# Turning y by a transposing transfer within SBUF, a stretch ahead, in place of TensorE transposes

## The chip, the core and the metric

The kernel runs on one core of one Trainium2 chip. The metric is the device time of one execution in microseconds. An execution's time is a little longer than the span of its instructions.

## The reference, cut to what matters

There are 8 batches, 5696 tokens and 128 channels. First comes a causal long convolution by FFT; its result is the y (and later x) of the second half. The second half turns y into phases, mixes over the tokens with two 5696 x 5696 matrices, and ends with a small channel product:

```
y     = irfft(rfft(x, 2S) * rfft(h, 2S))[:, :S]
theta = y @ w_theta
zr, zi = y * cos(theta), y * sin(theta)
u     = y + w_tok_r @ zr + w_tok_i @ zi        (the sums run over the tokens, per batch and channel)
out   = u + relu(u @ w_ch)
```

## The kernel before, in words

**Stages.** The first part, to about 400 us, does the FFT convolution and stores y with the channels on the partitions (`yt_hbm`). The second part mixes. A token tile is 128 tokens (45 tiles, the last with 64), and a *half tile* is one tile with 4 of the 8 batches: 128 x 512 values. The sum over the source tokens is cut in two passes. Pass 0 uses the tokens of tiles 0 to 21, pass 1 those of tiles 22 to 43; tile 44 is added at the end of pass 1's sums. After pass 0 the sums go to `cp_hbm` in HBM, and pass 1 loads them again (`addend`, L1091), adds its own, and puts out results.

**Pairs, products, stretches.** Output tiles are worked on in pairs (tt and 22 + tt), each with two halves, by seven products (`ORDER`: M3, M4, M5, M2, M1, M7, M6) in the manner of Strassen. Pair 0, and in pass 0 also pair 1, use four plain products; the lone last tile (`tt is None`) has its own short form. A pair's sum over 11 blocks j of source tokens is cut into four *stretches* of 3, 3, 3 and 2 blocks. In a stretch TensorE runs the seven products in turn (L1396: 6 matmuls for each block count of 3, 4 for 2). VectorE has made their weights before: it turns weights from a ring of six buffers (L972, `wt`) and adds or subtracts turned ones (L981, `out`). At the end of a pair VectorE adds the seven products into four tiles `c` (L1403, twelve additions), while it already makes the weights of the next pair's first stretch. GpSimd issues the weight loads into the ring (L669), each group once VectorE has read the buffer that it replaces.

**Background items.** Pass 1 needs the phases of tiles 22 to 44. They are made during pass 0, one half tile in each of the first three stretches of a pair, from pair 2 on. The list `spread` holds them as triples of functions; `bg_phase` (L989 to 1008) makes one for each half tile: tiles 24 to 33, 22, 23, 44, then 34 to 43, two halves each, 46 in all. After them come 12 items that turn left-over weights (`bg_left`), and in pass 1 the outputs (`u_stage`). Of a phase item
- `load` brings yT (channels on the partitions) from `yt_hbm`: SP, L995;
- `first` turns it with four TensorE transposes into a PSUM tile `tpz` (L1000), copies that with ScalarE into `yb` (L1002), and stores it to `y2_hbm` (L1003);
- `second` calls `phases_b`: four matmuls from yT to `theta_ps` (L552), ScalarE copies and sines (L554, L555, L572, L573, L576), VectorE's rounding (L556), VectorE's products of sine and cosine with `yb` (L587, L588), and four stores of z to `z_hbm` (SP, L611).

`yb` lies in the single buffer that `yt_room` gives (the profile calls it `ring`), so one y at a time is there. `bg_left` and `u_stage` use the same buffer. The PSUM tile `misc` is shared by `tpz`, `theta_ps`, `utp` and `v`.

**Outputs.** In pass 1 `u_stage` treats one finished half tile: ScalarE copies c to `ub` (L1049), SP turns it with a transposing transfer within SBUF (`dma_start_transpose`, L1052), TensorE multiplies by `w_ch` into `v` (L1063), VectorE adds (L1065), SP stores (L1068). The four last ones of the run are turned with TensorE instead (L1056, L1058).

**What sets the order.** `aside(first_of, second_of)` (inside the loop over the stretches) is called after each product and runs the `first` of the next item, then the `load` of the item after the next one, or the `second` of the current item. In Strassen stretches (L1420) `first` follows product 1, and `second` follows product 4 in pass 0, and product 6, or product 0 of the next stretch, in pass 1. Each engine executes its instructions in order; the framework's scheduler chooses that order ahead of time for TensorE, ScalarE and SP, and for VectorE outside of a few hand-ordered sections. SP issues all stores and most loads named here, in one queue.

**Pass change.** At the end of pass 0 the b tiles are loaded again from `z_hbm` and combined on VectorE (L880). Pass 1 starts with pair 0 (plain), then the lone last tile (L1273, four short stretches), then pair 1. The outputs of pair 0 and of the lone tile are the first five `u_stage` items.

Of the kernel before, what the change touches and what calls it, by code (L numbers as in the profile page):

```python
# [23 lines left out]
def kernel(  # L24
# [13 lines left out]
    P = 128  # L38
# [899 lines left out]
    def open_mixing():  # L938

        nonlocal bp, cp, wlp, ybp  # L940
        xa.close()
        bp, cp, wlp, ybp = (ctx.enter_context(tc.tile_pool(name=name, bufs=bufs, reuse_waits="tile"))
                            for name, bufs in (("bpool", 1), ("cpool", 1), ("wlpool", 2), ("ybpool", 3)))
        load_b(0, NJ - 2, bp)
        sides["cs"] = [addend(0, n, t, h) for n, (t, h) in enumerate(((0, 1), (22, 0), (0, 0), (22, 1)))]
        load_b(0, NJ - 1, bp)
        spread.extend(bg_phase(t, h) for t in list(range(24, 34)) + [22, 23, 44] + list(range(34, 44)) for h in range(2))
        spread.extend(bg_left(g) for g in range(0, NT, 4))
        spread[0][0]()
        spread[1][0]()  # L950

    for j in range(NJ):
        owed += [(j, k, lambda j=j, k=k: sum_ops(bts_of[0][j])[k]()) for k in range(5)]
# [35 lines left out]
    def bg_phase(t, h):  # L989
        st = {}  # L990
        m = min(P, S - t * P)

        def load():
            st["yT"] = yT = ybp.tile([P, 4, P], BF16, tag="yb", name="yT")
            nc.sync.dma_start(yT[:, :, :m], yt_hbm[:, 4 * h:4 * h + 4, t * P:t * P + m])  # L995

        def first():
            tpz = mps.tile([P, 4, P], BF16, tag="misc", name="tpz")
            for b in range(4):
                nc.tensor.transpose(tpz[:m, b, :], st["yT"][:, b, :m], ident_bf)  # L1000
            st["yb"] = yb = yt_room()
            nc.scalar.activation(yb[:m], tpz[:m], AF.Copy)  # L1002
            nc.sync.dma_start(half(y2_hbm, t, h)[:m], yb[:m].rearrange("p b d -> p (b d)"))  # L1003

        def second():
            phases_b(t, st["yb"], 4 * h, 4, st["yT"][:, :, :m], cp, mps, "misc", nc.vector,
                     tags=where_bg["tags"], m=m)
        return load, first, second

    def bg_left(g):  # L1010

# [28 lines left out]
            nc.sync.dma_start(wl_hbm[:, g:g + n, :m], wls[:, :n, :m])  # L1040
        return load, first, nothing

    def u_stage(ti, h, c, m):
        st = {}

        def first(tags=("misc", "misc", None)):
            st["tags"] = tags
            ub = ybp.tile([P, 4, D], BF16, tag="yb", name="ub")
            nc.scalar.activation(ub[:m].rearrange("p b d -> p (b d)"), c[:m], AF.Copy)  # L1049
            if not tags[2]:  # L1050
                st["uts"] = uts = yt_room()
                nc.sync.dma_start_transpose(uts, ub.rearrange("p b d -> p (b d)"))  # L1052
                return
            utp = mps.tile([P, 4, P], BF16, tag=tags[0], name="utp")
            for b in range(4):
                nc.tensor.transpose(utp[:, b, :m], ub[:m, b, :], ident_bf[:m, :m])  # L1056
            st["uts"] = uts = cp.tile([P, 4, P], BF16, tag=tags[2], name="uts")
            nc.scalar.activation(uts[:, :, :m], utp[:, :, :m], AF.Copy)  # L1058

        def second():  # L1060
            v = mps.tile([P, 512], F32, tag=st["tags"][1], name="v")
            for b in range(4):
                nc.tensor.matmul(v[:m, b * D:(b + 1) * D], st["uts"][:, b, :m], w_ch_sb,  # L1063
                                 start=True, stop=True)
            nc.vector.scalar_tensor_tensor(c[:m], v[:m], 0.0, c[:m],  # L1065
                                           op0=ALU.max, op1=ALU.add)
            for h_, p0, p1 in (((0, 0, 64), (1, 64, P)) if ti == NT - 1 else ((h, 0, m),)):
                nc.sync.dma_start(  # L1068
                    bass.AP(tensor=out.tensor, offset=out.offset + ti * P * D + 4 * h_ * S * D,
                            ap=[[D, p1 - p0], [S * D, 4], [1, D]]),  # L1070
                    c[p0:p1].rearrange("p (b d) -> p b d", b=4))
        return nothing, first, second
# [36 lines left out]
    def finish(p, ti, h, c, m=P):  # L1109
        if p == 0:  # L1110
            nc.sync.dma_start(half(cp_hbm, ti, h)[:m], c[:m])
        else:
            spread.append(u_stage(ti, h, c, m))

    zl_of = {0: None}

# [82 lines left out]
    for i, (k, p, tt, j0, s0, nj) in enumerate(stretches):  # L1199
# [40 lines left out]
                in_place(j)  # L1240
        if woven:
            nxt, step = nxt
        def aside(first_of, second_of):
            nonlocal second
            if first_of and spread and (p == 1 or (tt > 1 and not end_of_pair)):
                where_bg["tags"] = ("c2", "c3") if j0 + s0 == TJ else ("red", "mag")
                _, first, second = spread.pop(0)
                first()
                if len(spread) > 1:
                    spread[1][0]()  # L1250
            if second_of and second is not None:
                second()
                second = None

        if tt is None:
            if p:
                aside(False, True)
                aside(True, False)
            if first_of_pair:
                q = M1 if p else M3  # L1260
                ps = mps.tile([P, 512], F32, tag=f"m{q}", name=f"m{q}")
                c_last = addend_last(p)
            a1, a2, sa = a
            terms = ((sa, M2, a2, M4), (a1, M3, sa, M5))
            for j in range(nj):
                jj = j0 + s0 + j
                for r in range(2):
                    b = [x[:, r, :] for x in bts[jj]]
                    st_ = jj == 0 and r == 0
                    sp_ = jj == NJ - 1 and r == 1 and zl is None  # L1270
                    for k_ in range(2):
                        for h, t in enumerate(terms):
                            nc.tensor.matmul(ps[64 * h:64 * h + 64], t[2 * k_][:, j, :64, r], b[t[2 * k_ + 1]],  # L1273
                                             start=st_ and k_ == 0, stop=sp_ and k_ == 1)
            if p:
                for f in {0: (lambda: safe(NJ - 2),), TJ: (lambda: safe(NJ - 1),),
                          2 * TJ: (lambda: in_place(NJ - 2), lambda: in_place(NJ - 1))}.get(j0 + s0, ()):
                    f()
            if end_of_pair:
                if zl is not None:  # L1280
                    wl = wl_room()
                    nc.sync.dma_start(wl[:, :64], wl_hbm[:, NT - 1, :64])
                    for h in range(2):
                        nc.tensor.matmul(ps[64 * h:64 * h + 64], wl[:, :64], zl[h], start=False, stop=True)
                c, c0 = c_last
                nc.vector.tensor_add(c, c0, ps)
                finish(p, NT - 1, 0, c)
            continue
# [54 lines left out]
        if classic:  # L1343
            for n in range(4):
                for j in range(nj):
                    last = product(a, j0 + s0 + j, j, n, range(2))
                    if p == 0 and (n * nj + j) % 4 != 3:
                        sum_some(1)
                    if p == 0 and (n * nj + j) % 3:
                        y_some(1, last)  # L1350
                if end_of_pair and n % 2:
                    (c12, z12), (c21, z21), (c11, z11), (c22, z22) = cs
                    out_of = (((c11, z11, 0), (c12, z12, 1)), ((c21, z21, 2), (c22, z22, 3)))[n // 2]
                    for h, (c, z, m_) in enumerate(out_of):
                        if p:
                            nc.tensor.matmul(ms[m_], wl[n // 2], zl[h], start=False, stop=True)
                            nc.vector.tensor_tensor(c, z, ms[m_], op=add)
                            continue
                        if n == 1:
                            nc.tensor.matmul(ms[m_], ident_bf, z, start=False, stop=True)  # L1360
                        else:
                            for b in range(4):
                                nc.tensor.matmul(ms[m_][:, b * D:(b + 1) * D], z[:, b, :], ident_bf,
                                                 start=False, stop=(b == 3))
                        nc.scalar.activation(c, ms[m_], AF.Copy)
                aside(n == 0, n == 2 + p)
            if end_of_pair and woven:
                for n_ in range(7):
                    step(n_)
# [6 lines left out]
        else:  # L1376
# [14 lines left out]
            for n, q in enumerate(ORDER):  # L1391
# [9 lines left out]
                if end_of_pair:  # L1401
# [15 lines left out]
                    if woven:  # L1417
                        for n_ in {1: (0, 1), 2: (2,), 3: (3,), 4: (4,), 5: (5,), 6: (6,)}.get(n, ()):
                            step(n_)
                aside(n == 1, n == (6 if p and i + 1 < len(stretches) else 4) or p and n == 0)  # L1420
        if not end_of_pair:
            continue
        if i + 1 == len(stretches):
# [35 lines left out]
```

## Time and profile before

| | us |
|---|---|
| three runs, median (lowest to highest) | 1995.17 (1993.44 to 1997.12) |
| the profiled execution | 1982.45 |
| its span | 1980.2 |
| TensorE busy in the span | 1897.3 (96%) |
| VectorE busy | 1546.0 (78%) |
| ScalarE busy | 593.9 (30%) |
| GpSimd busy | 976.5 (49%) |
| pass 0's background items, first to last L1000 | 462.8 to 987.2 |
| one pair in pass 0, by its first theta matmul | 34.58 |

The profile lists instructions by source line, the engine, what is written and read, a count, and a duration; views of the trace give timelines, waits and landings of transfers. PE is TensorE's matmuls, PEld its weight loads, DVE is VectorE, ACT ScalarE, POOL GpSimd, and SPq the queue of SyncE. "[0.35 <-PE m]" behind a row means that the engine was idle for 0.35 us before it and that a matmul ended the wait. Matmuls overlap in the records, so their spacing tells more than their duration.

### The profile page before, as it was taken

The numbers are of one execution on the slowest core, as the hardware profiler recorded it, in microseconds if no ns is written. First come the engines' busy times: TensorE is split into PE (matmuls) and PEld (weight loads), VectorE is DVE, ScalarE is ACT, GpSimd is POOL, SyncE is SP. The second block draws the span as 40 slices with busy tenths as digits, with TensorE's granted clock in tenths as the row PEclk, the third lists the DMA queues.
The fourth block names the chain that finished last, engine by engine and source line by source line (L and its number), as shares of the span: only waits on it lengthen the run. The fifth ranks groups of instructions, "written<-read, shape, count | busy, mean of one in ns | idle before, by whom it ended". The sixth has DMA issues, their size and how long they took to land.

```text
span 1980.2 us, 40436 instructions
## 1 busy us (share of the span) xinstructions
PE 1897.3 (96%) x15247; PEld 1043.2 (53%) x15417; DVE 1546.0 (78%) x2855; ACT 593.9 (30%) x875; POOL 976.5 (49%) x1746
## 2 busy tenths in 40 slices
PE   5899998899999999999999997999999999999998
PEld 5799997544444444444444443444444444444444
DVE  8978787876888888888877677677687776777767
ACT  6999997812233333323310000000010000000001
POOL 8636414444453544536475645344535445354451
PEclk9999999999999999999999999999999999999999
DMA  9999959999898998989999899798989989899895
GB/s 110 79 102 145 102 113 243 261 224 167 176 178 173 175 174 159 186 170 178 172 167 162 139 300 174 111 168 142 171 151 170 164 144 165 148 165 172 144 168 115
DMA packets 534067, 323.13 MB, mean 163 GB/s; under 512 B 230311, under 2 KB 494663, under 8 KB 532887
## 3 DMA queue, kind: packets, MB, share of 16 engines
q0 software_dynamic: 322160, 156.41, 63.6%
q1 hardware_dynamic: 204544, 150.37, 28.5%
q10 hardware_dynamic: 7168, 13.76, 2.0%
q8 instruction: 121, 1.98, 0.4%
q14 instruction: 74, 0.61, 0.1%
HBM read 354.37 MB, written 90.29 MB: 225 GB/s over the span
## 4 chain that ended last, share of the span: by engine, by line
PE 63%; DMA 8%; DVE 5%; issue 2%; POOL 1%; SPq 0%; ACT 0%; DVEq 0%; ACTq 0%
PE m L1396 57%; PE m L1308 3%; DMA out_dram<-c 3%; DVE c L1403 2%; DMA c<-cp_hbm 1%; DMA b<-z_hbm 1%; DMA ring<-ub 1%; DVE wt L972 1%; PE v L1063 1%; PE m L1273 1%; PE m L1400 1%; PE tpz L1000 0%; PE misc L1308 0%; POOL ring L669 0%; PE theta_ps L552 0%
## 5 line engine op out<-in xcount | busy, mean ns | idle before, releaser
L669 POOL DMA_DIRECT2D ring<-in_moe_w_tok_i_dram x720 | 389.4, 552 | 660.5 <-DVE wt L972 571.0
L972 DVE STREAM_TRANSPOSE wt<-ring 128x384 f32<-128x384 f32 (+2 forms) x720 | 355.6, 521 | 124.0 <-PE m L1396 58.4
L669 POOL DMA_DIRECT2D ring<-in_moe_w_tok_r_dram x720 | 388.6, 553 | 118.0 <-DVE wt L972 39.7
L1396 PE MATMUL m<-b,wt 128*128 128x512 bf16 x1601 | 386.4, 380 | 4.1 <-DVE wt L972 1.7
L1049 ACT ACTIVATE ub<-c 128x512 bf16<-128x512 f32 x88 | 55.3, 630 | 768.9 <-DVE c L1403 659.4
L1403 DVE TENSOR_TENSOR c<-c,m 128x512 f32<-128x512 f32 x412 | 267.1, 670 | 21.7 <-DMA c<-cp_hbm 21.7
L1396 PEld LDWEIGHTS <-wt 128*128 128x128 bf16 x1804 | 173.3, 98 | 198.8 <-DVE wt L972 4.2
L139 POOL DMA_DIRECT2D x<-in_x_dram x128 | 99.4, 807 | 89.6 <-PE ps L255 82.9
L432 PE MATMUL ps<-r_u,uv 128*128 128x128 f16 x1024 | 125.1, 221 | 8.7 <-DVE ring L790 3.3
L432 PEld LDWEIGHTS <-uv 128*128 128x128 f16 x2048 | 120.4, 99 | 10.9 <-issue 7.1
L432 PE MATMUL ps<-r_v,uv 128*128 128x128 f16 x1024 | 124.8, 221 | 0.0
L408 DVE TENSOR_TENSOR uv<-xs,hs 128x1024 f16<-128x1024 f16 x192 | 117.1, 659 | 4.3 <-ACT xs L404 2.8
L1308 PE MATMUL m<-b,wt 128*128 128x512 bf16 x431 | 105.1, 379 | 3.6 <-DMA b<-zr_hbm 1.9
L404 ACT ACTIVATE xs<-ps 128x1024 f16<-128x1024 f32 x96 | 88.3, 991 | 3.3 <-PE ps L278 1.5
L1308 PEld LDWEIGHTS <-wt 128*128 128x128 bf16 x528 | 50.9, 98 | 62.6 <-issue 4.6
L554 ACT ACTIVATE red<-theta_ps,magic 128x512 f32<-128x512 f32 (+1 forms) x46 | 31.6, 687 | 129.7 <-PE theta_ps L552 109.2
L1002 ACT ACTIVATE ring<-tpz 128x512 bf16<-128x512 bf16 (+1 forms) x46 | 27.5, 597 | 140.2 <-PE tpz L1000 121.1
L880 DVE TENSOR_TENSOR b<-b 128x1024 bf16<-128x1024 bf16 x100 | 61.4, 681 | 3.9 <-DMA y_hbm<-b 3.9
L278 PEld LDWEIGHTS <-w_t 64*128 64x128 f16 x3240 | 56.1, 99 | 11.5 <-issue 5.6
L1065 DVE SCALAR_TENSOR_TENSOR c<-v,c 128x512 f32<-128x512 f32 x88 | 59.7, 680 | 2.1 <-PE v L1063 2.1
L572 ACT ACTIVATE mag<-red 128x512 f32<-128x512 f32 (+1 forms) x46 | 29.0, 631 | 93.2 <-DVE red L556 93.2
L255 PE MATMUL ps<-f_t,x 89*128 89x180 f16 x512 | 51.1, 242 | 3.3 <-DVE a__757 L260 0.9
(2934 smaller groups left out, 3555.0 us busy)
## 6 DMA issues: line engine op xcount, KB each, us to landing
ring<-in_moe_w_tok_r_dram POOLq DMA_DIRECT2D x352, 96.0 KB, 5.0
ring<-in_moe_w_tok_i_dram POOLq DMA_DIRECT2D x352, 96.0 KB, 5.1
ring<-in_moe_w_tok_r_dram POOLq DMA_DIRECT2D x352, 80.0 KB, 4.5
ring<-in_moe_w_tok_i_dram POOLq DMA_DIRECT2D x352, 80.0 KB, 3.9
cp_hbm<-c SPq DMA_DIRECT2D x88, 256.0 KB, 2.5
c<-cp_hbm SPq DMA_DIRECT2D x88, 256.0 KB, 4.2
out_dram<-c SPq DMA_DIRECT2D x88, 256.0 KB, 4.8
yy<-y_hbm SPq DMA_DIRECT2D x84, 128.0 KB, 2.4
```

The source lines that it names most:

```text
L139: nc.gpsimd.dma_start(x16[p0:p1, e, n0:n0 + 16, :HD], bass.AP(tensor=src.tensor, offset=src.offset + (p0 * N2 + n0) * D + dh * HD, ap=[[N2 ...
L278: nc.tensor.matmul(ps[:, e, j * HD:(j + 1) * HD], w_t2[rows, slot(e, c0 + j), N2 * (1 - ri):N2 * (3 - ri)], a_st["a"][rows, ri * K1 + c0 + ...
L404: nc.scalar.activation(xs[:, :, :, :CHK[c][1]], ps, AF.Copy)
L408: nc.vector.tensor_tensor(uv[e][:, :, :, c0:c0 + ck], xs_of[c][:, e:e + 1, :, :ck].to_broadcast([P, 2, HD, ck]), h_part(c), op=mult)
L432: nc.tensor.matmul(o, uv_t[e][:, r, d * K1:d * K1 + P], r_, start=(r == 0), stop=(r == 1))
L669: nc.gpsimd.dma_start(wb[32 * i:32 * i + 32, :ng, :nj * 64], bass.AP(tensor=a.tensor, offset=a.offset + row0 * S + p * H + i * QR + j0 * 6 ...
L880: return [lambda f=f, x=x: f(*x) for f, x in ((nc.vector.tensor_sub, (bt[M3], b12, b22)), (nc.vector.tensor_sub, (bt[M4], b21, b11)), (nc. ...
L972: nc.vector.transpose(wt.rearrange("p j t r -> p (j t r)").bitcast(F32).rearrange("p (j g t) -> p g j t", j=TJ, g=4)[:, :ng, :nj], wb[:, : ...
L1065: nc.vector.scalar_tensor_tensor(c[:m], v[:m], 0.0, c[:m], op0=ALU.max, op1=ALU.add)
L1308: ins = nc.tensor.matmul(ms[n // 2 * 2 + h], a[n][:, j, :, r], bts_of[p][jj][n % 2 * 2 + h][:, r, :], start=(n % 2 == 0 and jj == 0 and r ...
L1396: nc.tensor.matmul(ms[q], a[q][:, j, :, r], bts[jj][q][:, r, :], start=(jj == 0 and r == 0), stop=(jj == NJ - 1 and r == 1 and q not in left))
L1403: nc.vector.tensor_tensor(c, z, ms[q], op=op)
```

## The change

A phase item of a full tile gets a fourth function, `turned`: SP issues one transposing transfer from yT to the buffer `yb`. It is called through `turn_next` right after the `second` of the item before (for the first item, when the list is made). `first` then does nothing, and the y store moves into `second`. The two halves of tile 44 keep the TensorE way. `u_stage` takes an argument `turned`; the outputs of tiles 0, 22 and 44 (pair 0 and the lone tile) are now turned by four TensorE transposes and a ScalarE copy, all others, as before, by a transfer. In pass 1 `second` moves: to product 2 in plain stretches, to the end of each lone-tile stretch, and to product 4 in pair 1.

```diff
@@ open_mixing
         spread[0][0]()
         spread[1][0]()
+        spread[0][3]()
@@ bg_phase
+        def turned():
+            if m == P:
+                st["yb"] = yb = yt_room()
+                nc.sync.dma_start_transpose(yb, st["yT"].rearrange("p b n -> p (b n)"))
+
         def first():
+            if m == P:
+                return
             tpz = mps.tile([P, 4, P], BF16, tag="misc", name="tpz")
...
         def second():
+            if m == P:
+                nc.sync.dma_start(half(y2_hbm, t, h), st["yb"].rearrange("p b d -> p (b d)"))
             phases_b(t, st["yb"], 4 * h, 4, st["yT"][:, :, :m], cp, mps, "misc", nc.vector,
                      tags=where_bg["tags"], m=m)
-        return load, first, second
+        return load, first, second, turned
@@ u_stage
-    def u_stage(ti, h, c, m):
+    def u_stage(ti, h, c, m, turned=False):
...
-            if not tags[2]:
+            if turned:
                 st["uts"] = uts = yt_room()
                 nc.sync.dma_start_transpose(uts, ub.rearrange("p b d -> p (b d)"))
                 return
...
-            st["uts"] = uts = cp.tile([P, 4, P], BF16, tag=tags[2], name="uts")
+            st["uts"] = uts = cp.tile([P, 4, P], BF16, tag=tags[2], name="uts") if tags[2] else yt_room()
@@ finish
-            spread.append(u_stage(ti, h, c, m))
+            spread.append(u_stage(ti, h, c, m, turned=ti % 22 if ti < NT - 1 else 0))
@@ the loop over the stretches
+        def turn_next():
+            if spread and len(spread[0]) == 4:
+                spread[0][3]()
+
         def aside(first_of, second_of):
...
-                _, first, second = spread.pop(0)
+                _, first, second = spread.pop(0)[:3]
                 first()
                 if len(spread) > 1:
                     spread[1][0]()
             if second_of and second is not None:
                 second()
                 second = None
+                turn_next()
 
         if tt is None:
             if p:
-                aside(False, True)
                 aside(True, False)
...
             if p:
+                aside(False, True)
                 for f in {0: (lambda: safe(NJ - 2),), TJ: (lambda: safe(NJ - 1),),
...
-                aside(n == 0, n == 2 + p)
+                aside(n == 0, n == 2)
...
-                aside(n == 1, n == (6 if p and i + 1 < len(stretches) else 4) or p and n == 0)
+                aside(n == 1, n == (6 if p and tt > 1 and i + 1 < len(stretches) else 4))
```

## The prediction

> **What bounds the kernel now.** I read the busy time by stretch first, one stretch in the middle of each pass (from:to us, length, then busy us of PE, PEld, DVE, ACT, POOL with counts, granted clock, DMA share, GB/s):
>
> ```profile
> 600.00:950.00 350.00, 347.89 (x1761) 165.33 (x1796) 297.04 (x577) 112.11 (x180) 172.29 (x320) 1.00 0.92 173
> 1300.00:1650.00 350.00, 347.74 (x1703) 162.86 (x1737) 257.61 (x515) 25.21 (x40) 172.35 (x320) 1.00 0.97 159
> ```
>
> TensorE is busy 99.4% in both, at full clock; in pass 0 VectorE is busy 85% too. So whatever leaves TensorE in pass 0 should shorten the run, as long as VectorE and the transfers keep up. Two views say whether they do. First VectorE's timeline over one pair change (start, us), then TensorE's, both in pass 0:
>
> ```profile
> 701.03 0.43 DVE L981 TENSOR_TENSOR out__12914<-wt 128x512 bf16<-128x512 bf16 x1 [0.35 <-PE m L1396]
> 702.00 0.65 DVE L587 TENSOR_TENSOR red<-red,ring 128x512 bf16<-128x512 f32 x1
> 710.28 0.54 DVE L981 TENSOR_TENSOR out__13050<-wt 128x768 bf16<-128x768 bf16 x1
> ...
> 719.78 0.69 DVE L587 TENSOR_TENSOR red<-red,ring 128x512 bf16<-128x512 f32 x1 [0.50 <-ACT red L573]
> 727.41 0.69 DVE L587 TENSOR_TENSOR red<-red,ring 128x512 bf16<-128x512 f32 x1 [0.28 <-ACT red L573]
> 736.57 0.65 DVE L587 TENSOR_TENSOR red<-red,ring 128x512 bf16<-128x512 f32 x1
> ```
>
> ```profile
> 709.46 0.39 PE L1000 MATMUL tpz<-ident_bf,yT 128*128 128x128 bf16 x4
> 709.69 0.59 PE L1396 MATMUL m<-ring,out__13040 128*128 128x512 bf16 x2
> 710.98 0.59 PE L1396 MATMUL m<-ring,out__13050 128*128 128x512 bf16 x2
> ```
>
> From 701.03, which TensorE released, VectorE works without a gap to the end of out__13050 at 710.82; TensorE starts on it at 710.98. **At the change of pairs VectorE is 0.16 us ahead of TensorE, no more.** L587 is the first reader of yb; call its three executions in a pair M1 (719.78), M2 (727.41), M3 (736.57; in the pair before, 702.00). M3 stands at the head of that tight run.
>
> The third place is the pass change, by the waits of TensorE from 1195 to 1245 us (total us, times, longest) and the busy time of a stretch in it:
>
> ```profile
> PE v L1063 <- DMA ring<-ub: 11.1, 3, 4.7
> ```
>
> ```profile
> 1201.24:1241.02 39.78, 28.15 (x173) 12.82 (x174) 25.39 (x51) 3.04 (x5) 19.57 (x37) 0.91 1.00 144
> ```
>
> TensorE waits 11.1 us for transposing transfers there, and its clock is 0.91.
>
> **The change, part by part.**
>
> *Transposes leave TensorE.* 44 half tiles lose four L1000 each. The next matmul starts 0.23 us after a group (709.46 to 709.69), 0.22 elsewhere: 44 x 0.22 = 9.7 us. A pair takes 34.58 us and has three groups: 33.92 without them. One of the three lies inside the tight run: TensorE would take 9.95 - 0.22 = 9.73 us where VectorE takes 9.79, so VectorE decides and a pair cannot go much below 34.0. The 44 copies on ScalarE (0.60 each) cost nothing now (32% busy) and save nothing.
>
> *The transposing transfer.* Its price stands in pass 1, where 85 run; 78 of them:
>
> ```profile
> L1052 SPq DMA_TRANSPOSE ring<-ub x78: 1188/1190/2044, 1266.3 to 1948.8; - x78
> ...
> DMA to landing us min/median/max: 2.3/5.5/7.5
> ```
>
> It holds SP's queue 1.19 us and lands after 5.5. Between weight loads it lands in 2.3 to 2.5; beside them, 5.96 on average, 1.37 more than the weight loads issued in the 1.2 us before it. The y store L1003 of pass 0 lands only 0.12 later than such loads. So under load a transposing transfer is some 1.25 us slower than a plain one.
>
> *Where it stands on SP.* From the order of the changed program: the four z stores, the transfer, the next item's y store, the next yT load, then z stores again. SP before (start, us):
>
> ```profile
> 720.50 1.09 SPq L611 DMA_DIRECT2D z_hbm<-red  x2
> 721.69 1.19 SPq L611 DMA_DIRECT2D z_hbm<-mag  x2
> 722.96 0.54 SPq L1003 DMA_DIRECT2D y_hbm<-ring  x1
> 723.59 0.42 SPq L995 DMA_DIRECT2D yT<-yt_hbm  x1
> ```
>
> The transfer for item 2 takes the place at 722.96, that is M1 + 3.18. It lands L2 later and M2 waits for it; SP waits as well, because the y store stands right behind it and reads what it writes. Then y store, yT load (1.1 us with gaps) and four z stores (2.46) go out before the transfer for item 3: landing + 3.6. M3 cannot start before M1 + 3.18 + L2 + 3.6 + L3. From M3 to the next M1 is VectorE's own work, 17.78 us (702.00 to 719.78, one idle of 0.50). The transfer for item 1 is issued at a pair's end, over 15 us before M1: free. Behind its y store stand the four cp_hbm stores, which wait for c additions until 713.6 anyway, and a yT load that is due a stretch later. So a pair takes
>
> 24.56 + L2 + L3, or 34.0 if that is more; before, 34.58.
>
> M2's lateness alone is absorbed (VectorE has 4.6 us of gaps between M1 and M3); M3's is not, since VectorE's following sums and c additions are what TensorE waits for.
>
> *L2 and L3.* Lower ends: what the y stores in these places took, 5.54 and 4.62 on average (13 normal pairs), sum 10.16. Upper: 1.25 more each, 12.66. One thing pulls down: in the changed order VectorE reads the weight buffer that releases the next load just ahead of M2, not at 722.96, so fewer loads follow the transfer for item 2; they then fall on item 3's. I take 5.4 + 6.0 = 11.4, the middle: 35.96 us a pair, +1.38. Fourteen pairs have both transfers: +19.3 us (ends +2 and +37). The pair with tile 44, which stays on TensorE, and the last group save 0.8.
>
> *Start.* The first transfer waits on SP for its yT (landing 13.3 us after issue at 410.50), and the y stores of 414.8 to 420.2 queue behind it. VectorE waits for one of them until 427.1, so it may be 2 us late, but it also waits 2.0 for weights at 439.7 and 4.0 for TensorE at 464.6. I cost it at 0; without that cover 3.
>
> *Pass change.* Five outputs get four transposes and a ScalarE copy in place of a transfer: 5 x 0.22 = +1.1 on TensorE. The 11.1 us of waits go, and so does the slow clock (0.5 in the trace from 1220.1 to 1226.9 and 1240.6 to 1244.0, about 4.5 us by L1273 at 0.43 against 0.22 a pair). What is late next: each v and the next utp share the tile misc, so the transposes wait for L1065 on VectorE, some 0.3 to 1 us each; and VectorE has 25.4 us of work in these 39.8, so no more than 14.4 can go. I take -12 (ends -14 and -10). Moving `aside` in other stretches of pass 1 changes no count.
>
> **Sum:** +19.3 - 0.8 + 0 - 12 = +6.5 us. The profiled execution took 1982.45 us (span 1980.2, 2.25 around it), 12.7 less than the median of the runs, 1995.17; I put the difference on the median: **2001.7 us**. About 4 us (0.2%) is what a measurement of this kernel can tell from no change.
>
> The Trainium skill ("Advanced Engine Details and Errata", section "X-Bar Transpose (TRN2)") says that transposing transfers on this chip are as fast as regular ones. The trace agrees between bursts (2.3 us), not under load; its result is the first rival.
>
> **Rivals.**
>
> 1. *A transposing transfer lands like a plain one.* For: equal when the queues are empty. Against: the 1.25 us under load. L2 + L3 = 10.16, a pair 34.72: +2 - 0.8 - 12 to -14 = -11 to -13, 1982 to 1984. Chance 0.20, nearly all faster.
> 2. *The landings are hidden.* For: pass 1 gives its transfers 8.7 us before v and TensorE loses almost nothing there. Against: here M2 follows the issue by 4.45. It needs L2 + L3 under 9.4; then a pair takes 34.0: 14 x -0.58 = -8.1, -0.8, -12 = -21, 1974. Chance 0.14. This is the case of the other sign; it decides at L2 + L3 = 10.9, where the sum is zero.
> 3. *Full price under load on both*, 12.66: +37 - 0.8 - 10 = +26, 2021. For: every loaded row of pass 1. Chance 0.20.
> 4. *The pass change gives little*, because L1065 is late and misc stays taken: -4 in place of -12, +14.5, 2010. Against: VectorE idles 14 us of the 39.8 there. Chance 0.06.
>
> My forecast, L2 + L3 between 10.8 and 12, holds 0.40: 0.13 of it within 4 us, the rest slower.
>
> **Numbers.** Faster by over 0.2%: 0.19 + 0.14 = 0.33. Same: 0.14. Slower: 0.53. The range runs from between rivals 2 and 1 to rival 3: 1978 to 2022.
>
> **What would show it.** Right: L587 waits for the transfer ring<-yT; M1 to M3 grows from 16.79 to about 18.2; pairs take about 36 us; TensorE idles some 2 us at each pair start behind L981; no v waits between 1195 and 1245. Wrong: pairs of 34.0 with M1 to M3 unchanged (rival 2), landings below 5.2 in the bursts (rival 1), or PE still idle at the pass change (rival 4).

## The result, and the profile after

The changed kernel takes **2042.37 us** (median of 6 runs, 2033.15 to 2051.51), the one before 1994.31 (6 runs, 1991.96 to 1997.14): a ratio of **1.0238, 95% interval 1.0209 to 1.0267**, 42 to 53 us slower. The profiled execution took 2042.65 us (span 2040.9). The forecast was 2001.7 with a range up to 2022: the sign was right, the size far too small.

The same stretch of pass 0 that was shown of before, by the same view (busy us of PE, PEld, DVE, ACT, POOL with counts, granted clock, DMA share, GB/s):

```profile
600.00:950.00 350.00, 325.65 (x1541) 146.29 (x1540) 266.78 (x523) 89.13 (x142) 157.97 (x295) 0.98 0.99 167
```

TensorE has fallen from 99.4% to 93%, and every other engine is less busy too: all wait for something. VectorE's waits from 510 to 1050 us (total us, times, longest) name it; the second row, from the page's costliest groups (count, busy and mean, then idle time and its releaser), shows a wait that is not in the first list because it came earlier:

```profile
DVE red L587 <- DMA ring<-yT: 90.7, 26, 4.9
```

```profile
L1418 DVE TENSOR_TENSOR c<-yy,m 128x512 f32<-128x512 bf16 x80 | 51.0, 678 | 6.1 <-DMA z_hbm<-mag 6.0
```

Before, no L587 waited for a transfer; the one row of waits that L587 had over the same stretch was

```profile
DVE red L587 <- ACT red L573: 11.4, 28, 0.5
```

Now 26 wait for one, two for each of 13 pairs, 3.5 us each. One pair shows how (VectorE, then SP's queue, then TensorE; start, us):

```profile
676.85 0.69 DVE L587 TENSOR_TENSOR red<-red,ring 128x512 bf16<-128x512 f32 x1 [0.50 <-ACT red L573]
...
686.44 0.69 DVE L587 TENSOR_TENSOR red<-red,ring 128x512 bf16<-128x512 f32 x1 [2.58 <-DMA ring<-yT]
...
697.55 0.69 DVE L587 TENSOR_TENSOR red<-red,ring 128x512 bf16<-128x512 f32 x1 [4.44 <-DMA ring<-yT]
698.16 0.69 DVE L588 TENSOR_TENSOR mag<-mag,ring 128x512 bf16<-128x512 f32 x1
698.76 0.68 DVE L1418 TENSOR_TENSOR c<-yy,m 128x512 f32<-128x512 bf16 x1
699.36 0.42 DVE L982 TENSOR_TENSOR out__12455<-wt 128x512 bf16<-128x512 bf16 x1
```

```profile
678.75 1.19 SPq L611 DMA_DIRECT2D z_hbm<-mag  x2
679.99 1.41 SPq L1001 DMA_TRANSPOSE ring<-yT  x1
686.37 0.33 SPq L1015 DMA_DIRECT2D y_hbm<-ring  x1
686.80 0.38 SPq L996 DMA_DIRECT2D yT<-yt_hbm  x1
687.27 1.16 SPq L611 DMA_DIRECT2D z_hbm<-red  x2
688.52 1.18 SPq L611 DMA_DIRECT2D z_hbm<-mag  x2
689.80 1.33 SPq L1001 DMA_TRANSPOSE ring<-yT  x1
697.48 0.34 SPq L1015 DMA_DIRECT2D y_hbm<-ring  x1
```

```profile
699.84 1.04 PE L1411 MATMUL m<-b,out__12455 128*128 128x512 bf16 x4 [2.62 <-DVE out__12455 L982]
...
704.35 0.61 PE L1411 MATMUL m<-ring,out__12574 128*128 128x512 bf16 x2 [0.89 <-DVE out__12574 L982]
...
706.48 0.60 PE L1411 MATMUL m<-ring,out__12584 128*128 128x512 bf16 x2 [0.60 <-DVE out__12584 L982]
```

M1 is at 676.85. The transfer for item 2 goes out at 679.99, lands 6.36 us later, and M2 starts at 686.44; the y store, queued behind it, goes out at 686.37. The transfer for item 3 goes out at 689.80, lands 7.66 us later, and M3 starts at 697.55. Behind M3 stands out__12455, a sum of the last stretch's weights, for which TensorE waits 2.62 us; 0.89 and 0.60 follow at the start of the next pair: 4.1 us at this change of pairs.

The pass change is better, as its busy time shows, before and after, from the last group of c additions in pass 0 to the first of a full pair in pass 1:

```profile
1160.31:1261.57 101.26, 88.01 (x439) 39.67 (x445) 74.64 (x144) 3.04 (x5) 46.39 (x86) 0.95 0.98 203
```

```profile
1219.84:1309.58 89.74, 87.38 (x466) 39.50 (x465) 74.78 (x144) 5.80 (x10) 46.02 (x86) 1.00 1.05 225
```

It takes 11.5 us less at the same busy time; no v waits for a transfer, and the granted clock goes from 0.95 to 1.00.

**By stages.** The spans can be cut at VectorE's c additions, whose groups mark the pairs (all in us; three profiled executions of the kernel before and two of the changed one; two of the former and one of the latter are from the experiments):

| kernel | up to the first background pair's c | 16 pairs of pass 0 | pass change | pass 1 |
|---|---|---|---|---|
| before | 492.8, 496.3, 497.8 | 554.5, 554.4, 554.3 | 101.3, 99.2, 99.4 | 718.7, 721.4, 728.8 |
| changed | 497.4, 501.8 | 609.4, 607.3 | 89.7, 89.4 | 731.3, 728.3 |

The pairs left out here, at the end of pass 0, take 113.0 in all five. The two middle stages repeat within about 2 us and hold the change: +54.0 and -10.4 on the means, +43.6, inside the measured 42 to 53. The outer two scatter, and the next section asks whether the change moves them.

### The profile page after: what moved, and what is told of

Same layout as the page of the kernel before. It is cut to its first block, busy times and chain, and to the rows that moved or that the text cites. A ratio compares the mean times of both kernels' runs of the same rounds, so it can differ in the third digit from the quotient of the medians.

```text
span 2040.9 us, 40235 instructions
## 1 busy us (share of the span) xinstructions
PE 1918.1 (94%) x15261; PEld 1033.7 (51%) x15261; DVE 1543.2 (76%) x2855; ACT 570.6 (28%) x836; POOL 975.3 (48%) x1746
## 5 line engine op out<-in xcount | busy, mean ns | idle before, releaser
L1411 PE MATMUL m<-b,wt 128*128 128x512 bf16 x1640 | 395.0, 384 | 2.1 <-DVE wt L973 2.0
L1418 DVE TENSOR_TENSOR c<-c,m 128x512 f32<-128x512 f32 x412 | 267.5, 673 | 31.4 <-DMA c<-cp_hbm 31.2
L139 POOL DMA_DIRECT2D x<-in_x_dram x128 | 99.2, 795 | 88.6 <-PE ps L255 82.1
L1323 PE MATMUL m<-b,wt 128*128 128x512 bf16 x440 | 106.8, 380 | 5.6 <-DMA b<-zr_hbm 3.8
L587 DVE TENSOR_TENSOR red<-red,ring 128x512 bf16<-128x512 f32 (+1 forms) x46 | 31.8, 692 | 100.9 <-DMA ring<-yT 91.2
L1418 DVE TENSOR_TENSOR c<-yy,m 128x512 f32<-128x512 bf16 x80 | 51.0, 678 | 6.1 <-DMA z_hbm<-mag 6.0
L1411 PE MATMUL m<-ring,wt 128*128 128x512 bf16 x164 | 54.1, 415 | 0.6 <-DVE wt L973 0.6
```

The costliest lines, as they stand in the source:

```text
L139: nc.gpsimd.dma_start(x16[p0:p1, e, n0:n0 + 16, :HD], bass.AP(tensor=src.tensor, offset=src.offset + (p0 * N2 + n0) * D + dh * HD, ap=[[N2 ...
L1323: ins = nc.tensor.matmul(ms[n // 2 * 2 + h], a[n][:, j, :, r], bts_of[p][jj][n % 2 * 2 + h][:, r, :], start=(n % 2 == 0 and jj == 0 and r ...
L1411: nc.tensor.matmul(ms[q], a[q][:, j, :, r], bts[jj][q][:, r, :], start=(jj == 0 and r == 0), stop=(jj == NJ - 1 and r == 1 and q not in left))
L1418: nc.vector.tensor_tensor(c, z, ms[q], op=op)
```

## The experiments

The theory: two landings in each pair are not covered, M2 and M3 wait for them, and the landing of a transposing transfer is longer than I took it. The rivals: the transfers cost by being there, as load on the queues; the place on SP is to blame and not the form of the transfer; pass 1 loses by the moved calls. "A pair" below is the mean of 12 ordinary ones of pass 0 (without the first, that with tile 44, and the last two), between c additions: 34.58 before, 38.39 changed.

**The outputs' part alone.** The kernel before with the u_stage part and the moved calls:

```diff
@@ bg_phase and open_mixing as before; u_stage, finish, aside as changed
-            if not tags[2]:
+            if turned:
```

> Only the outputs' part of the change (u_stage, its argument, and the moved calls of aside in pass 1); the y of the background phases is turned by TensorE as in the kernel before. By the trace of the changed kernel the stretches from the last pair of pass 0 to the first full pair of pass 1 gave back 11.5 us (its lead over the kernel before fell from +59.5 to +48.0 us by the first c additions). If that part stands by itself, this kernel takes 11 to 12 us less than the one before, near 1983, with pairs of 34.58 in pass 0. Rival: the 12.5 us that the changed kernel's profiled execution lost again in pass 1 (c waiting for loads from cp_hbm) belong to the moved calls of aside. Then this kernel loses them too and ends near 1994, with pairs over 35.5 in the second half of pass 1.

It took 1987.33 us, ratio 0.9968 (0.9943 to 0.9993). Pairs of 34.58, a pass change of 88.8, pass 1 726.7. The gain at the pass change stands by itself: 11 us on the mean of the three profiles of before. Pass 1 was 8 us longer than in the first profile of before, which left the rival open, and by the ratio the kernel gained only 1 to 11 us.

**Two buffers for yb.** The transfers go out earlier; number and size stay:

```diff
+        def other_room():
+            return cp.tile([P, 4, P], BF16, tag="yy2", name="yb2")
...
                 first()
+                if j0 + s0 == 0:
+                    turn_next(0, other_room)
...
                 second = None
-                turn_next()
+                if j0 + s0 != TJ:
+                    turn_next(int(j0 + s0 == 0))
```

> The changed kernel, but with a second place for yb (the item of a pair's second stretch uses the tile yy2, which is free then): the transfer for item 2 goes out at the change of pairs and the one for item 3 right behind item 1's z stores, so that each has over 12 us ahead of its reader. As many transfers, the same sizes. Theory (the loss is the uncovered landing of two transfers in each pair): the waits of L587 for ring<-yT vanish, M1 to M3 is 16.8 again, a pair takes 34.0, the kernel gains some 8 us in pass 0 against the one before, and with 11.5 at the pass change it ends near 1975. Rival (a transposing transfer among the weight loads costs by itself, as load on the queues): the pairs stay at 36 to 38 with VectorE waiting for weights instead, 2015 to 2040.

It took 1989.23 us, 0.9965 (0.9934 to 0.9996). The L587 rows of one pair, M1, M2, M3 and the next M1:

```profile
655.59 0.69 DVE L587 TENSOR_TENSOR red<-red,ring 128x512 bf16<-128x512 f32 x1 [0.50 <-ACT red L573]
662.53 0.65 DVE L587 TENSOR_TENSOR red<-red,yb 128x512 bf16<-128x512 f32 x1
671.78 0.65 DVE L587 TENSOR_TENSOR red<-red,ring 128x512 bf16<-128x512 f32 x1
689.57 0.69 DVE L587 TENSOR_TENSOR red<-red,ring 128x512 bf16<-128x512 f32 x1 [0.51 <-ACT red L573]
```

No wait for a transfer is left, and M1 to M1 is 33.98 us. Ten of the 12 pairs take 33.97 or 33.98. The transfers issued in the bursts still land in 5.8 to 7.5 us, now unnoticed. So what costs is a landing that is not covered, and not the load that the transfers put on the queues. The whole time missed the expected 1975 by 14 us. Pass 0 gained 4 us in place of 8, since the first step between c additions took 38.88 us against 37.44 and the 12 ordinary ones gave only 5.7, and the pass change gained 10; pass 1, with 731.6 us, was among the longer ones (see below).

**The transfer ahead of two z stores.**

```diff
@@ phases_b, behind the product of mag and y
+        if then is not None:
+            then()
@@ bg_phase, second
-                     tags=where_bg["tags"], m=m)
+                     tags=where_bg["tags"], m=m, then=turn_next)
```

> The changed kernel with one thing moved: the transfer for the next item is put right behind VectorE's last use of yb; by the order of the program two of the four z stores still stand ahead of it on SP, and two behind it. It should go out at M + 1.95 in place of M + 3.15. Theory (uncovered landing): with landings as in the changed kernel (6.5 and 6.9) M1 to M3 is 1.95 + 6.6 + 1.95 + 7.0 = 17.5, a pair 35.3 in place of 38.4: some 35 us less than the changed kernel, near 2005. Rival (load on the queues): nothing changes but the order, 2035 to 2045.

It took 2032.7 us, 1.0197 (1.0149 to 1.0245), a pair 37.12: better than the changed kernel by 1.3 us a pair, not by 3.1. The transfer for item 2 went out at M1 + 1.92, as expected; that for item 3 at M2 + 3.57. SP's own waits from 510 to 1040 us (L1007 is the transfer here, L1021 the y store) tell why:

```profile
SPq L1021 <- DMA ring<-yT: 111.9, 27, 5.5
...
SPq L1007 <- DMA y_hbm<-ring: 28.0, 23, 2.3
```

With one buffer the transfer overwrites what the y store of the item before still reads, so it waits until that store has landed. I had not priced this second hold. In the changed kernel itself SP's z stores fill most of that time (it waits 3.6 us in 6 such waits).

**No turning at all**, for the floor:

```diff
-                st["yb"] = yb = yt_room()
-                nc.sync.dma_start_transpose(yb, st["yT"].rearrange("p b n -> p (b n)"))
+                st["yb"] = st["yT"]
```

> The changed kernel without any turning of y for the 44 full half tiles: neither four TensorE transposes nor a transfer; the unturned yT is used and stored in place of y. This leaves out part of the computation and shows the floor. Both theories: no wait at L587, a pair takes 34.0 by VectorE's work (my prediction's bound) or less; near 1975. If pairs take 34.58 as before, TensorE's transposes cost nothing and the change had nothing to win in pass 0.

It took 1977.14 us, 0.9896 (0.9844 to 0.9948), a pair 33.98. That is the floor which VectorE's work sets: at the change of pairs TensorE now starts 0.06 us after VectorE has made the sum that it reads, in place of 0.17 before. The kernel with two buffers reaches it (mean 34.11). Three transposing transfers a pair that nobody waits for cost 0.13 us a pair here.

**A plain copy in the same place.**

```diff
-                nc.sync.dma_start_transpose(yb, st["yT"].rearrange("p b n -> p (b n)"))
+                nc.sync.dma_start(yb, st["yT"])
```

> The changed kernel with a plain copy within SBUF (yT to yb, 128 KB, 1 KB a partition) in the place of each of the 44 transposing transfers, so y stays unturned: part of the computation is left out. Everything else, the waits and their places in SP's queue too, is as in the changed kernel. There the two transfers inside a pair took 6.6 and 6.8 us to land, and a pair 38.45. Theory (the form of the transfer is what makes it dear): the copies land like the weight loads issued just ahead of them, 1.2 to 1.7 us sooner, 5.1 to 5.4 each; a pair takes 35.5 to 36, and the kernel some 2000 to 2010. Rival (the place is what makes it dear, behind bursts of weight loads): 6.3 to 6.8 again, a pair 38, 2035 to 2045.

It took 2001.14 us, 1.0057 (1.0026 to 1.0088), a pair 35.84, as the theory had it. One view, all executions of the line, of the changed kernel first and then of the plain copies (us from issue to landing in the last row of each):

```profile
L1001 SPq DMA_TRANSPOSE ring<-yT x44: 1190/1239/2134, 428.7 to 1042.1; - x44
...
DMA to landing us min/median/max: 2.3/6.0/7.9
```

```profile
L1001 SPq DMA_DIRECT2D ring<-yT x44: 487/549/979, 425.3 to 1001.4; - x44
...
DMA to landing us min/median/max: 1.9/4.8/6.9
```

For items 2 and 3 the plain copies landed in 5.78 and 5.12 us on average, the transposing transfers in 6.60 and 6.80 (13 pairs each): 10.90 against 13.40. So the form costs 2.5 us a pair here, and the pair is 2.55 shorter. The place costs the rest: even a plain transfer is not covered, and the pair stays 1.86 us above the floor of 33.98. That is more than the 0.60 that TensorE's transposes had cost, so the pair is 1.26 us longer than before (35.84 against 34.58).

**The y store freed of its wait.**

```diff
-                nc.sync.dma_start(half(y2_hbm, t, h), st["yb"].rearrange("p b d -> p (b d)"))
+                nc.sync.dma_start(half(y2_hbm, t, h), st["yT"].rearrange("p b d -> p (b d)"))
```

> The kernel of the run with the transfer ahead of z, but its y store reads yT in place of yb: as many stores of the same size, but none that reads what the transfer writes, so that SP never waits for the landing and the next transfer not for the store. It leaves out part of the computation, since the y that is stored is not turned. In the run with the transfer ahead of z the transfer for item 2 went out at M1 + 1.92, as expected, but that for item 3 at M2 + 3.57 in place of M2 + 1.95, and a pair took 37.1 in place of 35.3. Theory (what held it is the y store in front: it is issued after the landing, and the next transfer overwrites what it reads and so waits until the store has landed): item 3's goes out at M2 + 1.9 and a pair takes 1.92 + 7.1 + 1.9 + 6.65 + 0.2 + 17.83 = 35.6. Rival (it is the z stores' own wait or their issue that holds it): item 3's stays at M2 + 3.5 and a pair at 37.

It took 2039.67 us, 1.0246 (1.0189 to 1.0303), a pair 38.56. Neither came: item 3's transfer went out at M2 + 4.8 on average. The edit changed more than it was meant to. The scheduler put the freed store right behind a yT load, and SP stood there instead (L1002 is that load):

```profile
SPq L1002 <- DMA ring<-yT: 108.9, 25, 5.3
SPq L1021 <- DMA yT<-yt_hbm: 105.8, 38, 5.9
```

As a test of the y store's hold it is inconclusive; the wait row of the run ahead of z is the evidence. In the two pairs in which the transfer did go out at M2 + 1.9, the next steps by c additions are 35.07 and 33.98.

**The kernels again, and the parts of the outputs' change.**

> The kernel before, unchanged, for a second look at the stretches that the change does not touch. All five kernels profiled since took 8 to 15 us more in pass 1 (from its first full pair to the end) than the first profile of the kernel before, and 5 to 19 us more ahead of the first changed instruction. Theory (both vary from execution to execution, and that first profile was a short one, 1982.45 where the median is 1995): here too the part ahead of pass 0's first background item is 5 to 15 us longer and pass 1 5 to 12 us longer. Rival (the moved calls in pass 1 cost it): pass 1 is within 3 us of the first profile.

> The changed kernel, unchanged, for a second look. Theory (pass 0 loses by a fixed mechanism, the rest varies): pairs of 38.4 in pass 0 within 0.3, about 50 us lost there, 11 to 13 back at the pass change; ahead of pass 0 and in pass 1 the difference to the first profile is anywhere in 10 us either way.

The kernel before took 1986.42 us, the changed one 2041.82 (single runs; stages in the table above). The first of these spoke for the rival, with 721.4 for pass 1 (2.8 us above the first profile). The changed kernel's pairs were 38.36, as expected; it lost 53 us in them. So three more runs went to pass 1. Without the moved calls:

```diff
@@ the loop over the stretches: as before; u_stage and finish as changed
-                aside(n == 0, n == 2)
+                aside(n == 0, n == 2 + p)
```

> The kernel before with the first five outputs turned by TensorE, and nothing else: the calls of aside in pass 1 stay where they were, y is turned by TensorE. Question: pass 1, from its first c addition of a full pair to the end, took 727 to 736 us in the eight profiles with the whole outputs' part and 719 and 721 in the two of the kernel before, though from there on every engine has the same instructions in the same order. Theory A (the shorter pass change itself, the state of the transfers in which pass 1 is entered, costs it): the pass change gives 11 to 13 us back, pass 1 takes 727 or more; 1985 to 1991. Theory B (the moved calls cost it): pass 1 takes 718 to 722 and the whole gain stays, near 1980. Theory C (chance): pass 1 anywhere from 718 to 735.

```diff
@@ u_stage and finish as before; only the calls moved
-                aside(n == 0, n == 2 + p)
+                aside(n == 0, n == 2)
```

> The kernel before with only the calls of aside moved in pass 1; all outputs turned by transfers, y by TensorE. By theory B (the moved calls cost pass 1 its 8 us) pass 1 takes 727 or more, while the pass change gives nothing or up to 4 us, its waits for the transfers being there still: 1995 to 2005. By theory A pass 1 takes 718 to 722 and the kernel stays within 5 us of the one before. By theory C anything from 718 to 735.

> The kernel before, a third look at the length of pass 1 in it. By theories A and B 718 to 722 again; by theory C it may take 725 or more.

| kernel | median us, ratio (interval) | pass change | pass 1 |
|---|---|---|---|
| outputs without moves | 1986.0, 0.9978 (0.9950 to 1.0006) | 88.0 | 721.1 |
| moves alone | 2004.63, 1.0065 (1.0042 to 1.0089) | 104.7 | 728.8 |
| before, third profile | 1995.47, one run | 99.4 | 728.8 |

The third profile of the kernel before took 728.8 us in pass 1, as much as some of the changed ones. So the stage scatters by 10 us in one and the same kernel, and from 719 to 736 over all profiles, with every engine's instructions in the same order; VectorE's c additions wait there for loads from `cp_hbm`, 21.7 to 48.2 us in all. One profile of each kernel cannot settle the question. But that chance is all of it (theory C) is not shown either. The five profiles without the moved calls took 718.7 to 728.8 us, 723.4 on the mean; the nine with them took 726.7 to 735.9, 730.6 on the mean. And the moved calls alone make the kernel 8 to 18 us slower by their interval, of which the pass change holds 4.7 in their one profile. So they may well cost pass 1 some 7 us (theory B), where the forecast had put them at nothing; how they would do so is open. Open as well is why the outputs without moves are only between 10 us faster and 1 us slower, when their trace shows 12 us at the pass change.

**The two gains together.** The kernel with two buffers, its calls of aside as before:

```diff
@@ the loop over the stretches, from the kernel with two buffers
-                aside(n == 0, n == 2)
+                aside(n == 0, n == 2 + p)
```

> The two parts that gained, together: y turned by transfers with two places for yb (pairs of 33.97 in pass 0), and the first five outputs turned by TensorE without the moved calls (88.0 us for the pass change). The thirteen kernels profiled so far vary by chance ahead of pass 0's background items (493 to 511) and in pass 1 (719 to 736); what lies between is fixed to 2 us. There this kernel should save 4 us by the background items and 12 us at the pass change against the kernel before: 16 us, 0.8%, near 1977. If transfers and the shorter pass change hinder each other, the pass change takes 90 or more, as in the run with two buffers.

It took 1983.95 us, 0.9946 (0.9923 to 0.9969): 16 pairs in 550.3, pass change 88.5, so 4.1 and 11.5 us by the stages. It is faster than both kernels, by 6 to 15 us than the one before; the 16 us of the stages lie just outside, and the expected 1977 was missed by 7 us.

## Why the prediction was wrong in size

**The chain was right.** Fourteen pairs had both transfers, as forecast, but in the first of them M2 waited only 0.6 us and M3 not at all, so 13 count. The parts of the chain, on the mean of these 13: the transfer for item 2 at M1 + 3.25 (forecast 3.18), that for item 3 at M2 + 3.77 (about 3.5), M3 to the next M1 17.84 (17.78), each M 0.09 after its landing. These terms come to 0.5 us a pair more than forecast. M1 to M3 is 20.6 in place of 18.2.

**The step that failed is "I take 5.4 + 6.0 = 11.4".** It measured 6.60 + 6.80 = 13.40, above even the upper end of 12.66. The price of the form, twice 1.25 us from pass 1, was right in the sum: 2.5 us over plain copies in the same places, though unevenly, 0.83 and 1.68. Two other things were wrong. The base, what the y stores took in those places (5.54 and 4.62), was 0.74 us too low: plain copies there take 5.78 and 5.12. And the middle of the bounds was taken in place of the upper one, another 1.26. The reason for it was that fewer weight loads would follow the transfer for item 2. They did: 4.8 were issued in the 6 us behind it on average, against 7.2 behind the y store before. But it landed after 6.60 us all the same, not after 5.4. The rows under load were the nearest ones, and they gave rival 3, which still fell short by the base. Of the 2.4 us by which a pair exceeds the forecast, 2.0 are this; over 13 pairs the whole excess is 32 us.

The Trainium skill ("Advanced Engine Details and Errata", section "X-Bar Transpose (TRN2)"), which calls transposing transfers as fast as regular ones, holds nearly between the bursts (item 1's land in 2.4 us, plain copies in 2.1, medians of 14) and not in them (13.40 against 10.90 us for the two of a pair). Rival 1, which stood on it, would not have come out even with plain copies: 35.84 a pair, not 34.72.

**The first pair was priced like the others.** The first step between the pairs' c additions lost 9.0 us in one profile and 7.4 in the other, some 4 more than the 12 ordinary ones. There the second c addition waits 6.0 us for the landing of a z store of item 2, the row of L1418 above, where it had waited 1.9 before: the tiles c2 and c3 are lent to that item, and its lateness comes out there, outside the chain.

**The stall stood elsewhere than I said**: mostly at the last stretch's last product (2.62 of 4.1 us), less at the start of the next pair. Both follow M3.

**Right**: the floor of 34.0 a pair (33.98 without turning); the pass change (forecast -12, ends -14 and -10; -10.4 on the means, with the slow clock gone; rival 4 is out); the start, as far as its scatter lets one see (the first background pair's c came at 493 to 511 us). **Too simple**: that the moved calls cost nothing (4.7 us at the pass change when alone, and perhaps more in pass 1), and that the tile-44 pair and the last ones save 0.8 (-0.2 there, +0.35 in the last two).

That the profiled 1982.45 us was a short execution is right too: the later profiles of the same kernel spent 3 to 5 us more ahead of the change and 3 to 10 more in pass 1.

## What to carry to other kernels

Moving a step from an engine to a transfer trades a short cost in the stream for a landing: find its first reader, count from the release of the buffer to that reader, and compare with the landing times of the same form of transfer under the same load, at their upper end. Where the buffer is single, its release includes every store that still reads it, so a second buffer may be worth more than an earlier place in the queue. And test the cut by stages: here the stages that the change touches repeat within about 2 us, while whole runs of one kernel scatter by over 20.

## What the runs showed of the hardware

- A transposing transfer of 128 KB within SBUF held SP's queue 1.24 us (median), a plain one 0.55. Under the weight loads it landed 0.83 and 1.68 us later than a plain one in the same two places; between bursts they took 2.4 and 2.1 (medians).
- The same program with the same order of instructions took 719 to 729 us in pass 1 in three profiled executions, and its first part varied by 5. Over all 14 profiles the first yT load, ahead of which every engine's instructions stand in the same order, went out at 410.5 to 430.0 us.
- With the gaps of up to 3.6 us in TensorE's stream the granted clock of the stretch in pass 0 was 0.98 in place of 1.00, and at the pass change it rose from 0.95 to 1.00 when the waits of up to 4.7 us went.
